# A new fixed order of steps for the opening of a fused attention and feed-forward kernel

## The chip, the cores and the metric

The kernel runs on one core of one Trainium2 chip. A core has TensorE (PE in the profile; its weight loads are shown apart as PEld), VectorE (DVE), ScalarE (ACT), GpSimd (POOL), and SyncE (SP), whose queue issues most of the transfers here. Each engine takes its instructions in order and waits on semaphores for the others. The metric is the device time of one execution in microseconds.

## The reference

```
def _attn_ref(q, k, v):                      # 8 batches, 8 heads, 576 positions, 64 wide
    scores = scale * np.matmul(q, k.transpose(0, 1, 3, 2))
    ...
    masks = np.stack([mask_local if h < H // 2 else mask_strided for h in range(H)], axis=0)
    scores = np.where(masks[None, :, :, :], scores, -1000000000.0)
    ...
    attn = attn / (np.sum(attn, axis=-1, keepdims=True) + 1e-09)
    return np.matmul(attn, v).astype(np.float32)

def _moe_ref(x, w1, w2, w3, w_out):          # x: 4608 tokens x 512; w1..w3: 512 x 768; w_out: 768 x 512
    h = np.maximum(np.maximum(x @ w1, x @ w2), x @ w3)
    return (h @ w_out).astype(np.float32)
```

Half of the heads attend to the last 32 positions, the other half to the positions that agree modulo 32. The result, with the heads side by side, is the `x` of a feed-forward block whose hidden value is the maximum of three products.

## The kernel before

The attention is done in 32 units: a unit is one batch and one pair of heads, in the order strided, strided, local, local. The feed-forward block is done in nine chunks of 512 tokens. A float32 product is made of three products of parts that PE reads faster (`float32r`): every operand is split into a high part and a low rest, for `x` and the hidden value as for the weights. The weights come as pairs of 32-bit words (the host gives float64) and are converted on the chip, in 24 tiles (three matrices by six column blocks, then six of `w_out`).

Up to the end of chunk 0 the order of all work is fixed by a table, `OPENING`. Each entry is a letter and a number, and the steps are recorded on their engines in the order of the table; `pin` keeps that order. The letters:

- **S** n: scores of unit n on PE (lines 248 and 266). **X** n: mask and minus the maximum, DVE (289, 290). **E** n: exponential, ACT (294). **N** n: sums, reciprocal, product and transpose, five instructions on DVE (302 to 307).
- **V** n: value products of unit n on PE into the PSUM tile `o_ps` (lines 333 and 374). **H** n: its high part, copied from `o_ps` by ACT (391) into `xh`. **L** n: its rest, DVE (395), into `xl`. Units 0 to 3 make the `x` of most of chunk 0 (batch 0); 4 to 7 belong to batch 1.
- **A** n: first step of the conversion of weight tile n, two ACT instructions (146, 147) into a tile `work`, of which there are three, and one on POOL (148). **B** n: three DVE instructions (160, 163, 166); the first writes two of the four banks of `o_ps`, in columns that the value products don't use, and the second reads them. **C** n: ACT makes the high part (174), POOL the low one by subtraction (175), which ends the use of `work`.
- **F** n: one of 18 input products of chunk 0 on PE, 12 matmuls (line 410) into one of two banks `f_ps`; weight tile n is needed. **M** n: what takes its result out of the bank: a copy on ACT (421) for every third n, a maximum on DVE (423) for the others, and after the third a cast on ACT (426) and a subtraction on POOL (427). F n + 2 waits for M n.
- **O** n: one of four output products, 18 matmuls (436), into the same two banks; **Q** n: copy on ACT and store (441, 442).

The four banks of `o_ps` are shared between V, H, L and B, and accesses by different engines to one bank are kept in the order of the table, whether their columns meet or not.

The 24 loads of weights and the first loads of `q`, `k` and `v` are issued ahead of the table; S n and V n with n of 4 or more issue the loads of unit n + 2. Behind the table, for chunks 1 to 8, a scheduler places the steps.

Of the kernel before, what the change touches and what calls it, by code (L numbers as in the profile page):

```python
# [43 lines left out]


OPENING = """
S0 X0 S1 E0 N0 A0 X1 B0 E1 S2 V0 N1 A1 B1 H0 X2 A2 L0 S3 V1 E2 C0 A3 H1 C1 B2 X3 N2 E3 L1 V2 A4 H2 N3 L2
S4 V3 B3 C2 A5 C3 B4 H3 L3 X4 A6 E4 B5 C4 F0 M0 F1 F2 B6 C5 M1 N4 C6 A7 M2 B7 F3 S5 A8 X5 A9 C7 B8 M3 F4
F5 V4 E5 B9 C8 A10 A11 M4 C9 M5 F6 N5 A12 F7 B10 M6 B11 C10 F8 H4 S6 A13 C11 B12 C12 A14 L4 M7 B13 A15
B14 C13 C14 M8 F9 V5 F10 M9 A16 X6 A17 B15 M10 C15 B16 E6 F11 F12 B17 A18 C16 M11 B18 C17 A19 M12 F13  # L50
A20 C18 A21 N6 F14 M13 B19 S7 B20 H5 C19 F15 C20 M14 F16 M15 B21 A22 F17 L5 A23 M16 C21 B22 C22 M17 V6
B23 X7 C23 O0 Q0 E7 O1 Q1 H6 O2 N7 L6 Q2 V7 H7 O3 Q3 L7
"""


# [518 lines left out]
```

## Time and profile before

| | us |
|---|---|
| median of 3 runs | 737.13 (736.61 to 740.75) |
| profiled execution | 736.63 |
| its span, first to last instruction | 734.9 |
| PE busy | 700.3 (95%) |
| DVE busy | 315.7 (43%) |
| ACT busy | 171.5 (23%) |
| POOL busy | 124.0 (17%) |

The shares are means over a span with two very different parts: the opening, where all engines work on the conversion, the first units and chunk 0, and the rest, where PE is busy without a break. Times below are counted from the span's start.

### The profile page before, as it was taken

The page shows a single profiled execution, that of the slowest core. Times are in us where ns is not written, and L with a number is a line of the kernel's source. Part 1 is how long each engine was busy: PE and PEld are TensorE (multiplying, and loading weights), DVE is VectorE, ACT ScalarE, POOL GpSimd, SP SyncE. Part 2 cuts the span into 40 slices and gives each one's busy share as a digit, 9 for nine tenths or more (in the row PEclk, how much of TensorE's full clock was granted, in tenths as well). Part 3 has the DMA queues.
Part 4 walks back from the last instruction along what each step waited for, and adds up shares of the span by engine and source line. Part 5 has one row for each costly group of instructions (what it writes and reads, how often), then busy time and mean ns, then how long its engine had stood idle before and what let it go on. Part 6 is the DMA issues. An engine that isn't in the chain of part 4 may idle for free.

```text
span 734.9 us, 18756 instructions
## 1 busy us (share of the span) xinstructions
PE 700.3 (95%) x8448; PEld 563.2 (77%) x8448; DVE 315.7 (43%) x527; ACT 171.5 (23%) x346; POOL 124.0 (17%) x129
## 2 busy tenths in 40 slices
PE   6387998999999999999999999999999999999997
PEld 5266766888788887888788878887888788888885
DVE  5677997444425441555145523553344401101110
ACT  2435654222212111122111212121122211111111
POOL 4235665011101110011001100101011101200110
PEclk9999999999999999999999999999999999999999
DMA  8996111311231122222222211222210010000001
GB/s 240 283 312 239 46 40 45 106 54 53 62 120 54 54 62 88 73 66 62 73 68 57 92 58 62 60 75 66 88 54 21 12 48 1 0 29 29 1 1 57
DMA packets 35807, 55.34 MB, mean 75 GB/s; under 512 B 5200, under 2 KB 18512, under 8 KB 35728
## 3 DMA queue, kind: packets, MB, share of 16 engines
q1 hardware_dynamic: 30016, 44.19, 20.5%
q10 hardware_dynamic: 5712, 9.96, 3.7%
q8 instruction: 66, 1.08, 0.6%
q14 instruction: 13, 0.11, 0.0%
HBM read 44.70 MB, written 9.44 MB: 74 GB/s over the span
## 4 chain that ended last, share of the span: by engine, by line
PE 82%; DVE 2%; POOL 1%; issue 1%; ACT 0%; DVEq 0%; POOLq 0%; ACTq 0%
PE f_ps L410 55%; PE f_ps L436 20%; PE s_ps L266 4%; PE o_ps L333 2%; PE o_ps L363 2%; DVE work L166 1%; POOL wNone L175 1%; DVE work L163 0%; DVE o_ps L160 0%; ACT work L441 0%; POOL work L148 0%; DVE h_max L423 0%; DVE s_ps L305 0%; POOL hl L427 0%; DVE s_ps L302 0%
## 5 line engine op out<-in xcount | busy, mean ns | idle before, releaser
L410 PE MATMUL f_ps<-xh,w 128*128 128x512 f32 x1296 | 417.1, 396 | 6.8 <-DVE h_max L423 5.9
L410 PEld LDWEIGHTS f_ps<-xh,w 128*128 128x128 f32 x1296 | 244.9, 189 | 61.7 <-DVE h_max L423 7.4
L410 PE MATMUL f_ps<-xl,w 128*128 128x512 f32 x648 | 254.2, 392 | 0.7 <-DVE xl L395 0.7
L427 POOL TENSOR_TENSOR hl<-h_max,hh 128x512 fp32r<-128x512 f32 x54 | 70.0, 1296 | 534.9 <-ACT hh L426 534.9
L423 DVE TENSOR_TENSOR h_max<-f_ps,h_max 128x512 f32<-128x512 f32 x108 | 74.5, 689 | 187.9 <-PE f_ps L410 187.9
L436 PE MATMUL f_ps<-wNone,hh 128*128 128x512 f32 x432 | 140.9, 396 | 1.8 <-ACT wNone L174 0.7
L410 PEld LDWEIGHTS f_ps<-xl,w 128*128 128x128 f32 x648 | 122.7, 189 | 24.9 <-DVE xl L395 1.0
L436 PEld LDWEIGHTS f_ps<-wNone,hh 128*128 128x128 f32 x432 | 81.0, 188 | 20.5 <-ACT work L441 1.3
L436 PE MATMUL f_ps<-wNone,hl 128*128 128x512 f32 x216 | 85.0, 394 | 0.0
L426 ACT CAST hh<-h_max 128x512 fp32r<-128x512 f32 x54 | 33.5, 621 | 205.7 <-DVE h_max L423 205.7
L395 DVE TENSOR_TENSOR xl<-o_ps,xh 128x320 fp32r<-128x320 f32 (+11 forms) x96 | 28.3, 350 | 80.0 <-ACT xh L391 80.0
L441 ACT COPY work<-f_ps 128x512 f32<-128x512 f32 x36 | 20.9, 586 | 123.9 <-PE f_ps L436 123.9
L266 PEld LDWEIGHTS s_ps<-qk_t 64*32 64x32 f32 x3200 | 35.1, 111 | 18.6 <-issue 16.6
L421 ACT COPY h_max<-f_ps 128x512 f32<-128x512 f32 x54 | 31.7, 587 | 74.7 <-PE f_ps L410 43.0
L436 PEld LDWEIGHTS f_ps<-wNone,hl 128*128 128x128 f32 x216 | 40.6, 188 | 8.1
L266 PE MATMUL s_ps<-qk_t 64*32 64x18 f32 (+1 forms) x3200 | 40.8, 209 | 3.7 <-DMA qk_t<-in_kT 2.0
L294 ACT ACTIVATE s_ps<-s_ps 128x640 f32<-128x640 f32 (+2 forms) x32 | 20.3, 635 | 85.6 <-DVE s_ps L290 85.1
L287 DVE TENSOR_TENSOR s_ps<-s_ps,mpair 128x576 f32<-128x576 f32 x12 | 9.2, 767 | 67.8 <-PE s_ps L266 67.8
L333 PEld LDWEIGHTS o_ps<-pt,v_t 32*64 32x64 f32 x1344 | 18.5, 141 | 19.3 <-DVE xl L395 10.4
L333 PE MATMUL o_ps<-pt,v_t 32*64 32x64 f32 (+1 forms) x1344 | 22.0, 238 | 10.8 <-DVE xl L395 10.3
L391 ACT CAST xh<-o_ps 128x320 fp32r<-128x320 f32 (+11 forms) x96 | 24.4, 330 | 32.9 <-PE o_ps L333 25.4
L307 DVE STREAM_TRANSPOSE pt<-s_ps 128x640 f32<-128x640 f32 (+2 forms) x32 | 31.3, 979 | 0.7
(49 smaller groups left out, 341.9 us busy)
## 6 DMA issues: line engine op xcount, KB each, us to landing
out<-work ACTq DMA_DIRECT2D x36, 256.0 KB
w<-in_w SPq DMA_DIRECT2D x17, 512.0 KB
qk_t<-in_qT SPq DMA_DIRECT2D x28, 288.0 KB
qk_t<-in_kT SPq DMA_DIRECT2D x28, 288.0 KB
v_t<-in_v_str SPq DMA_DIRECT2D x48, 128.0 KB
v_t<-in_v_loc SPq DMA_DIRECT2D x48, 96.0 KB
wNone<-in_w_out SPq DMA_DIRECT2D x6, 512.0 KB
v_t<-in_v_str SPq DMA_DIRECT2D x16, 72.0 KB
```

Source lines behind the costliest of these rows:

```text
L266: pin(nc.tensor.matmul(s_ps[32 * j : 32 * (j + 1), h, k1 : k1 + w], t[hs, q0 : q0 + 32], t[hs, k0 : k0 + w], start=not first, stop=not fir ...
L307: pin(nc.vector.transpose(pt[:, :, : nm * at], s_ps[:, :, : nm * at]))
L333: pin(nc.tensor.matmul(o[h * D : (h + 1) * D, j, 32 * max(m, 0) : 32 * max(m, 0) + width], v[js, h, m + 1, :], pt[js, h, m * TK + 32 : m * ...
L391: pin(nc.scalar.copy(out=hi, in_=src))
L395: pin(nc.vector.tensor_tensor(out=lo, in0=src, in1=hi.bitcast(F32), op=ALU.subtract))
L410: pin(nc.tensor.matmul(f_ps, w[:, kc, :], x[:, kc, :], start=(kc == 2 and n == 0), stop=(kc == 1 and n == 2)))
L421: pin(nc.scalar.copy(out=a, in_=f_ps))
L423: pin(nc.vector.tensor_tensor(out=a, in0=f_ps, in1=a, op=ALU.max))
L426: pin(nc.scalar.copy(out=hh, in_=a))
L427: pin(nc.gpsimd.tensor_tensor(out=hl, in0=a, in1=hh.bitcast(F32), op=ALU.subtract))
L436: pin(nc.tensor.matmul(f_ps, h[:, ts], w, start=(j == 0 and n == 0), stop=(j == NJ - 1 and n == 2)))
L441: pin(nc.scalar.copy(out=o_sb, in_=hs.pop((c, "out", t))))
```

## The change

The table `OPENING` gets a new order. The steps are the same, each once, and so are their instructions; nothing else in the file differs.

```
 OPENING = """
-S0 X0 S1 E0 N0 A0 X1 B0 E1 S2 V0 N1 A1 B1 H0 X2 A2 L0 S3 V1 E2 C0 A3 H1 C1 B2 X3 N2 E3 L1 V2 A4 H2 N3 L2
-S4 V3 B3 C2 A5 C3 B4 H3 L3 X4 A6 E4 B5 C4 F0 M0 F1 F2 B6 C5 M1 N4 C6 A7 M2 B7 F3 S5 A8 X5 A9 C7 B8 M3 F4
...
+A0 S0 X0 E0 N0 S1 X1 B0 E1 S2 A1 N1 C0 X2 V0 A2 B1 B2 H0 C1 S3 A3 L0 X3 V1 E2 E3 N2 C2 H1 L1 V2 N3 A4 S4
+H2 A5 L2 B3 C3 X4 E4 B4 C4 V3 H3 N4 L3 F0 A6 B5 A7 F1 C5 B6 M0 C6 M1 A8 S5 B7 X5 C7 A9 B8 E5 F2 F3 C8 M2
...
 """
```

In the part that is not printed, V4 to F6 read `V4 E5 B9 C8 A10 A11 M4 C9 M5 F6` before, and now `V4 A10 A11 M3 F4 B9 C9 B10 F5 C10 H4 M4 A12 S6 M5 X6 A13 F6`. M8 to F11 read `M8 F9 V5 F10 M9 A16 X6 A17 B15 M10 C15 B16 E6 F11` before, and now, from V5 on, `V5 A15 A16 F9 M8 B14 C14 B15 A17 B16 M9 C15 B17 A18 C16 A19 F10 M10 F11`. The last conversion, `B23 ... C23`, and O0 read `V6 B23 X7 C23 O0` before, and now `M17 B23 X7 C23 H6 O0`. On PE the same blocks follow each other up to F1; from there S5 stands before F2 and no longer before F4, S6 before F6 and no longer before F9.

How the order stands on the engines at three places. First DVE early in the fill, where the pair of line 395 is L0 and the three with `w_0_185` around it are B2:

```order
-L395 TENSOR_TENSOR xl<-o_ps,xh 128x512
-L395 TENSOR_TENSOR xl<-o_ps,xh 128x64
 L160 TENSOR_SCALAR o_ps<-work 128x2x256
 L163 SCALAR_TENSOR_TENSOR work<-w_0_185,o_ps 128x512
 L166 ISA work<-w_0_185,work 128x1024
+L395 TENSOR_TENSOR xl<-o_ps,xh 128x512
+L395 TENSOR_TENSOR xl<-o_ps,xh 128x64
```

L0 stood ahead of B2 and now stands behind it.

Then DVE later in the fill, with B3 (its last row first), B4 (`w_1_195`), the three rows of L3 and, with line 289 and 290, X4:

```order
 L166 ISA work<-w_1_193,work 128x1024
+L289 TENSOR_REDUCE mx<-s_ps 128x16
+L290 TENSOR_TENSOR s_ps<-s_ps,mx 128x2x8x18
 L160 TENSOR_SCALAR o_ps<-work 128x2x256
 L163 SCALAR_TENSOR_TENSOR work<-w_1_195,o_ps 128x512
 L166 ISA work<-w_1_195,work 128x1024
-L395 TENSOR_TENSOR xl<-o_ps,xh 128x480
-L395 TENSOR_TENSOR xl<-o_ps,xh 128x32
-L395 TENSOR_TENSOR xl<-o_ps,xh 128x64
-L289 TENSOR_REDUCE mx<-s_ps 128x16
-L290 TENSOR_TENSOR s_ps<-s_ps,mx 128x2x8x18
```

X4 now stands ahead of B4; L3 stands further on, behind the five instructions of N4, and V3 is recorded behind B4 and no longer ahead of B3.

Last DVE about V4, with B9 (`w_3_213`) behind B8 (its last row first), and M4 and M5 as the two of line 423:

```order
 L166 ISA work<-w_2_211,work 128x1024
-L160 TENSOR_SCALAR o_ps<-work 128x2x256
-L163 SCALAR_TENSOR_TENSOR work<-w_3_213,o_ps 128x512
-L166 ISA work<-w_3_213,work 128x1024
-L423 TENSOR_TENSOR h_max<-f_ps,h_max 128x512 x2
+L423 TENSOR_TENSOR h_max<-f_ps,h_max 128x512
 L302 TENSOR_REDUCE s_ps<-s_ps 128x2x8
```

B9 no longer stands here between B8 and a maximum: the one row of line 423 is M2, and M4 and M5 come later, behind B9 and B10.

## Rows read from the trace of the kernel before

**Rows 1.** Busy time by stretch: length, busy us of each engine, clock, DMA share, GB/s
```profile
core 0: us, PE busy (x) PEld busy (x) DVE busy (x) ACT busy (x) POOL busy (x), PEclk, DMA share, GB/s
0.00:44.41 44.41, 24.01 (x973) 19.18 (x973) 24.98 (x47) 14.30 (x28) 14.36 (x36) 1.00 0.92 277
50.58:117.72 67.14, 59.88 (x830) 47.15 (x828) 59.78 (x90) 39.10 (x71) 42.14 (x40) 0.97 0.32 111
117.72:138.77 21.05, 19.70 (x289) 15.43 (x284) 9.88 (x19) 6.35 (x16) 3.82 (x3) 1.00 0.30 89
138.77:734.90 596.13, 591.63 (x6360) 477.97 (x6352) 215.20 (x362) 109.24 (x226) 61.77 (x48) 1.00 0.18 54
```

**Rows 2.** Who PE waited for, 0 to 138.77 us: total, times, longest
```profile
PE f_ps L410 <- DVE h_max L423: 5.9, 5, 3.0
```

**Rows 3.** Timeline of the fill: start, us, engine, line, instructions, idle before and releaser
```profile
20.66 0.70 ACT L391 CAST xh<-o_ps 128x512 fp32r<-128x512 f32 x2 [1.66 <-DVE work L163]
...
22.68 0.67 ACT L146 ACTIVATE work<-w 128x512 f32<-128x512 f32 x1 [1.32 <-DMA w<-in_w]
...
23.42 0.61 POOL L148 TENSOR_SCALAR work<-work 128x512 f32<-128x512 f32 x1 [4.30 <-ACT work L146]
...
23.78 2.22 PE L374 MATMUL o_ps<-pt,v_t 18*64 18x18 f32 x128 [1.89 <-DVE xl L395]
...
28.69 0.69 DVE L160 TENSOR_SCALAR o_ps<-work 128x512 int32<-128x512 int32 x1 [4.96 <-ACT xh L391]
...
32.53 0.82 DVE L302 TENSOR_REDUCE s_ps<-s_ps 128x10 f32<-128x640 f32 x1
...
35.49 0.78 DVE L395 TENSOR_TENSOR xl<-o_ps,xh 128x512 fp32r<-128x512 f32 x2
...
36.33 1.65 PE L333 MATMUL o_ps<-pt,v_t 32*64 32x64 f32 x84 [10.32 <-DVE xl L395]
...
39.29 1.33 PE L248 MATMUL s_ps<-mstr,unit 128*128 128x144 f32 x4 [1.31 <-DVE pt L307]
...
42.83 1.65 PE L333 MATMUL o_ps<-pt,v_t 32*64 32x64 f32 x84
...
45.43 1.05 PE L410 MATMUL f_ps<-xh,w 128*128 128x512 f32 x2
...
49.21 0.87 DVE L395 TENSOR_TENSOR xl<-o_ps,xh 128x480 fp32r<-128x480 f32 x3
...
50.01 0.50 PE L410 MATMUL f_ps<-xl,w 128*128 128x512 f32 x1 [0.67 <-DVE xl L395]
...
50.35 0.62 PE L410 MATMUL f_ps<-xh,w 128*128 128x512 f32 x2
...
51.04 0.62 PE L410 MATMUL f_ps<-xh,w 128*128 128x512 f32 x2
```

**Rows 4.** Timeline around V4 and F6
```profile
67.34 1.44 PE L374 MATMUL o_ps<-pt,v_t 18*64 18x18 f32 x128
...
68.89 0.69 DVE L160 TENSOR_SCALAR o_ps<-work 128x512 int32<-128x512 int32 x1 [3.60 <-PE o_ps L374]
...
70.44 0.69 DVE L166 CUSTOM_DVE_ANT_0 work<-w,work 128x1024 uint16<-128x1024 uint16 x1
...
71.05 1.41 DVE L423 TENSOR_TENSOR h_max<-f_ps,h_max 128x512 f32<-128x512 f32 x2
...
71.79 0.77 PE L410 MATMUL f_ps<-xh,w 128*128 128x512 f32 x1 [3.01 <-DVE h_max L423]
```

**Rows 5.** Busy time by stretch, behind the longest wait of PE
```profile
71.85:75.25 3.40, 3.40 (x8) 2.72 (x9) 3.23 (x8) 1.87 (x3) 3.14 (x3) 0.50 0.23 62
```

**Rows 6.** Timeline and, last, group of line 166 on DVE, 0 to 138.77 us
```profile
97.04 1.28 POOL L175 TENSOR_TENSOR w<-work,w 128x512 fp32r<-128x512 f32 x1 [0.46 <-ACT w L174]
...
97.35 1.51 DVE L166 CUSTOM_DVE_ANT_0 work<-w,work 128x1024 uint16<-128x1024 uint16 x1
...
L166 DVE CUSTOM_DVE_ANT_0 work<-w,work 128x1024 uint16<-128x1024 uint16 x18 | 17.8, 989 | 2.0
```

More of the change, by code (lines that the diff above doesn't have):

```diff
@@ L46 @@
 OPENING = """
-S0 X0 S1 E0 N0 A0 X1 B0 E1 S2 V0 N1 A1 B1 H0 X2 A2 L0 S3 V1 E2 C0 A3 H1 C1 B2 X3 N2 E3 L1 V2 A4 H2 N3 L2
-S4 V3 B3 C2 A5 C3 B4 H3 L3 X4 A6 E4 B5 C4 F0 M0 F1 F2 B6 C5 M1 N4 C6 A7 M2 B7 F3 S5 A8 X5 A9 C7 B8 M3 F4
[L49 to L52, printed above, removed]
+A0 S0 X0 E0 N0 S1 X1 B0 E1 S2 A1 N1 C0 X2 V0 A2 B1 B2 H0 C1 S3 A3 L0 X3 V1 E2 E3 N2 C2 H1 L1 V2 N3 A4 S4
+H2 A5 L2 B3 C3 X4 E4 B4 C4 V3 H3 N4 L3 F0 A6 B5 A7 F1 C5 B6 M0 C6 M1 A8 S5 B7 X5 C7 A9 B8 E5 F2 F3 C8 M2
+N5 V4 A10 A11 M3 F4 B9 C9 B10 F5 C10 H4 M4 A12 S6 M5 X6 A13 F6 B11 B12 F7 M6 C11 L4 F8 C12 B13 E6 M7 A14
+C13 V5 A15 A16 F9 M8 B14 C14 B15 A17 B16 M9 C15 B17 A18 C16 A19 F10 M10 F11 C17 B18 F12 C18 M11 H5 M12
+N6 F13 A20 F14 L5 A21 B19 V6 C19 A22 M13 F15 B20 C20 M14 F16 M15 A23 F17 B21 M16 B22 C21 C22 S7 M17 B23
+X7 C23 H6 O0 E7 L6 N7 O1 Q0 O2 V7 Q1 H7 L7 O3 Q2 Q3
 """
```

## The prediction

> **What bounds the kernel now.** I read first the busy time in stretches cut at three events on PE: the first matmul of F0 (44.41 us), the first of F1 (50.58) and the first of O0 (117.72), with chunk 1 starting at 138.77 [rows 1]. From 138.77 to the end PE is busy for 591.6 of 596.1 us: nothing in this table of steps touches that part, because the program behind it is the same. So the change is worth what it takes from, or adds to, the 138.77 us before it, and it can do so only through the time in which PE waits, or runs slowly. PE's work is a fixed sum.
>
> Three parts of it are to be seen. In the fill (0 to F0) PE is busy for 24.0 of 44.4 us. From F1 to O0 it is idle for 67.14 - 59.88 = 7.26 us, and of these the list of waits gives 5.9 us, in five waits, to the running maximum M on DVE (line 423), which hands back one of the two banks of `f_ps` [rows 2]. From O0 to chunk 1 it is idle for 21.05 - 19.70 = 1.35 us.
>
> The timeline shows why. The value products V, their copies H and L, and the middle step of a weight conversion, B, share one PSUM tile, `o_ps`, and wait for each other in the order in which the table names them. H0 on ACT started at 20.66, released by line 163 of B1, although B1 has nothing to do with head pair 0; B2 on DVE stood from 23.7 to 28.69 waiting for the copies H1 that V1 has to precede [rows 3]. DVE is in order, so X3, N2 and L1 stood behind B2, and V2 on PE waited 10.32 us for L1. The same at V3: its products began at 42.83 and took 1.65 us, but B3 and B4 stand between V3 and L3, so the last operand of F0 was written from 49.21 on, and F0's matmul with it started at 50.01 [rows 3].
>
> **The change, part by part.** I walk the new order with the old durations. The loads are issued in the same order up to the last weight, so I keep their landings: the DMA share of the fill is 0.92 [rows 1], and no step moved there issues a load.
>
> *Fill.* B2 now stands ahead of H0. Its weight lands at 22.68 (A2 starts then, released by the DMA), POOL is done at 24.03 [rows 3]. B2's first two instructions, 0.69 each with small gaps, take 1.45: 25.5. H0 0.70: 26.2. L0 0.78: 27.0, so V1 starts near 27.1, which is 3.3 us *later* than its 23.78. But then nothing is in the way: behind L0 come X3 and N2. From B2's start at 28.69 to N2's start at 32.53 are 3.84 us and N2 lasts until 35.49, 2.96; in the new order B2 starts at 24.06, so N2 starts at 24.06 + 3.84 + 0.78 = 28.7 and ends at 31.6. V1 (2.22) and H1 end by 30.1 and are hidden. L1 0.78: V2 at 32.45 instead of 36.33, 3.9 us earlier. N3 follows (as long as N2), to 35.3, and frees the scores' bank for S4, which with its sequel took 42.83 - 39.29 = 3.54: 38.85. B3 fits in before that. X4, two of the five instructions of a block like N2 and on fewer columns, I take as 0.9; the first two parts of B4 are 1.45: 41.2. V3 waits for these, 41.25 to 42.8, and F0 starts at 42.8 instead of 44.41, **1.6 us** earlier. V3 is followed at once by H3 (0.7), and L3 comes behind N4 on DVE (41.9 plus at most N2's 2.96, plus L3's 0.87: 45.7). F0 needs L3 for its 11th matmul. In the old run a pair of F0's first matmuls took 1.05 us, against 0.62 for a pair from 50.35 on, where three starts are 0.69 apart, 0.23 each [rows 3]: that is the 1.2 GHz level, though the clock column has no record that early, with 0.43 a matmul (8 in 3.40 us) [rows 5]. I let the slow part last 3.5 us again, as behind the longest wait below: 8 matmuls until 46.3, four at 0.23 follow, and L3 is early. F1 starts at 47.3 instead of 50.58: **-3.3 us**, bounds -1.6 (only F0's start moves) and -4.
>
> *F1 to O0.* Work of PE here: 59.88, less what a slow clock cost. At 71.85 to 75.25 the granted clock is 0.50 (1.2 GHz), right behind the longest wait, with 8 matmuls in it [rows 5]; half of 3.40 is 1.7. So 58.2 at full clock. The longest wait, 3.01 us, is one chain: V4 on PE, 67.34 to 68.78; B9 on DVE waits for it, 68.89 to 71.13; the maximum M4, the first of the two of line 423, stands behind B9 and ends near 71.74; F6 needs the bank that M4 frees, 71.79 [rows 4]. In the new order M3 stands ahead of B9, and F4, F5 and S6 come between V4 and F6. Between V4 and F6 PE then has two F of 2.75 (12 times 0.23) and a score block (S4's 3.54 at the slow level, so about 1.8), over 7 us, against two conversions of 2.2 (68.89 to 71.05) to 2.7 and M4's 0.7 on DVE: covered, the wait goes to 0, and the clock should stay at 2.4 GHz. If that cover were gone, it would cost what it costs now, 3.0 + 1.7. S5 likewise goes between F1 and F2, about 1.8 us of PE work while DVE does B5 and the first maximum. What is late next: the new table lets M9 stand behind A17 on ACT, A17 behind C14 on POOL (three buffers named `work`), C14 behind the subtraction of M8, while PE has V5, F9 and F10 in that time. That is a series of about 0.7 (M8), 0.7 (its cast), 1.3 and 1.3 (two subtractions on POOL [rows 6]), 1.3 (A17, two of 0.67 [rows 3]) and 0.6 us (M9) and queueing, against about 7 of PE. I expect a wait ahead of F11 between 0 and 3.0 (the longest of its kind now) and take 2.4, and five small ones of 0.25 at V5, F9, F12, F13 and F15. Sum 3.65. 58.2 + 3.65 = 61.85 instead of 67.14: **-5.3 us**, bounds 0 (the idle time and the clock drop come back at other places) and -8.9 (all idle time and the clock's loss go).
>
> DVE must be able to follow: it has 59.78 busy us in the old stretch. In the new order N4 (at most 2.96) and B5 (2.2) are done before F1, so about 55 of 61.85: it fits, at 90%.
>
> *O0 to chunk 1.* The last conversions, B23 and C23, now stand before O0; the waits for them (1.35) go: **-1.3 us**, bounds 0 and -1.3.
>
> Sum: -3.3 - 5.3 - 1.3 = -9.9. The profiled execution has 736.63 us with a span of 734.90; 725.0 of span gives 726.7, and the median of the runs lies 0.5 above the profiled one: **727.2 us**.
>
> **The rule weighed against it.** The third instruction of B, line 166, takes 0.69 alone [rows 4], 0.99 on average over 18 of 24, and 1.51 where it starts inside a POOL subtraction: POOL 97.04 to 98.32, DVE 97.35 to 98.86, so it ends 0.54 after POOL does [rows 6]. The Trainium skill, page "SBUF — State Buffer", section "Who interferes with whom", says that VectorE and GpSimd share a pair of ports as an exclusive lock, and whoever issues second is fully blocked. The trace agrees here. By that rule the new order, which lets B follow on B with a C in between, might have every line 166 wait out a subtraction: I price this as the fourth rival, from the rows.
>
> **The rivals.**
> 1. *The waits only move.* The fill's gain stays, but DVE, ACT and POOL queues give PE as much to wait for from F1 on as now. For it: DVE at 90%, and M9 behind A17. Against it: the longest wait has a plain cause that the new order undoes. 737.1 - 3.3 = 733.8.
> 2. *Slower: the late V1 carries through.* If all behind V1 depends on V1 rather than on DVE, its 3.3 us stay: 737.1 + 3.3 = 740.4. The point that decides is whether V2 starts later than 36.33. Against it: V2 waited 10.32 us for DVE, not for V1, which ended at 26.0.
> 3. *No wait at F11*: 727.2 - 2.4 = 724.8. For it: the series and PE's work are about equal.
> 4. *The lock.* 18 times 1.51 - 0.99 adds 9.4 to DVE's 55 from F1 to O0: 64.4, past 61.85 by 2.5: 729.7. Against it: C's cast and subtraction are about 0.7 and 1.28 behind one line 166, and two of 0.69 stand ahead of the next, so a held one loses about 0.5, not 0.8.
>
> **How the numbers follow.** Chances: the forecast 0.66 (own range 725 to 730; its upper part has a clock drop at F11, 1.7 as above), waits only move 0.12, slower 0.05, no wait at F11 0.09, lock 0.08. The range 723.5 to 732.5 leaves out the slower case and most of rival 1. Half a per cent, 3.7 us, is about what a measurement of this kernel can tell from no change: faster is below 733.4. Forecast, 3, 4 and about half of rival 1 are faster, 0.89; the rest of rival 1 and a little of 2 the same, 0.07; slower 0.04.
>
> **What would show it.** Right: V1 near 27, V2 near 32.5, F0 near 43 and F1 near 47; no PE wait of 3 us from F1 to O0 but one up to 3 ahead of F11; no half clock after the start of the F steps; chunk 1 near 129. Wrong: V2 after 36, F0's 11th matmul waiting for L3, DVE without idle time from F1 to O0 and line 166 near 1.5 on average, or a half clock behind the wait at F11.

## The result, and the profile after

The changed kernel takes 729.33 us (median of 4 runs, 728.72 to 730.34) against 737.18 for the kernel before beside it: a ratio of 0.9885, with a 95% interval of 0.986 to 0.991. That is 2.1 us above the predicted 727.2 and inside its range. The profiled execution took 728.72 us with a span of 727.0, so 7.9 us of span are gone where 9.9 were forecast.

The busy time of the changed kernel in the same four stretches as [rows 1], cut at F0, F1, O0 and the start of chunk 1:

```profile
core 0: us, PE busy (x) PEld busy (x) DVE busy (x) ACT busy (x) POOL busy (x), PEclk, DMA share, GB/s
0.00:46.87 46.87, 21.88 (x972) 17.72 (x973) 30.90 (x58) 15.96 (x31) 15.69 (x38) 0.73 0.90 270
50.66:111.80 61.14, 58.12 (x830) 46.06 (x828) 56.00 (x84) 37.82 (x68) 40.36 (x39) 1.00 0.39 129
111.80:131.17 19.37, 19.37 (x288) 15.49 (x285) 8.12 (x17) 5.10 (x14) 2.75 (x3) 1.00 0.30 99
131.17:727.00 595.83, 591.63 (x6359) 477.83 (x6352) 215.18 (x362) 109.20 (x226) 61.78 (x48) 1.00 0.18 54
```

Set beside the sum of the prediction:

| stretch | before | after | change | predicted |
|---|---|---|---|---|
| start to F1 | 50.58 | 50.66 | +0.1 | -3.3 |
| F1 to O0 | 67.14 | 61.14 | -6.0 | -5.3 |
| O0 to chunk 1 | 21.05 | 19.37 | -1.7 | -1.3 |
| chunk 1 to the end | 596.13 | 595.83 | -0.3 | 0 |

The two stretches behind F1 gave a little more than forecast; the whole miss is in the fill, which gave nothing, outside the bounds of -1.6 to -4 that it had been given. F0 starts at 46.87 and not at 42.8. What PE waited for up to chunk 1 says where to look (in all, times, longest):

```profile
PE s_ps L266 <- issue: 6.3, 3, 4.4
PE o_ps L374 <- DVE xl L395: 6.1, 1, 6.1
PE o_ps L333 <- DVE xl L395: 3.3, 1, 3.3
...
PE o_ps L333 <- DVE work L163: 2.4, 1, 2.4
PE f_ps L410 <- ACT h_max L421: 1.9, 1, 1.9
PE o_ps L333 <- issue: 1.4, 1, 1.4
PE f_ps L410 <- DVE h_max L423: 0.7, 1, 0.7
```

The 10.3 us of V2 [rows 3] have become 6.1 at V1 and 3.3 at V2, the five waits for the running maximum [rows 2] one of 0.7 and one of 1.9 for M9 (predicted: 2.4 ahead of F11). But the top row has no engine to blame: for 4.4 us at a stretch PE stood in the middle of a step while it waited for nothing that the profile shows. The timeline of the fill, with the rows that answer to V2, S4 and V3 in [rows 3]:

```profile
31.87 1.26 PE L333 MATMUL o_ps<-pt,v_t 32*64 32x64 f32 x59 [3.29 <-DVE xl L395]
...
34.58 0.67 PE L333 MATMUL o_ps<-pt,v_t 32*64 32x64 f32 x25 [1.45 <-issue]
35.18 1.33 PE L248 MATMUL s_ps<-mstr,unit 128*128 128x144 f32 x4
...
36.89 1.16 PE L266 MATMUL s_ps<-qk_t 64*32 64x18 f32 x98 [0.38 <-DMA qk_t<-in_kT]
...
42.41 0.44 PE L266 MATMUL s_ps<-qk_t 64*32 64x18 f32 x30 [4.36 <-issue]
42.96 0.46 DVE L289 TENSOR_REDUCE mx<-s_ps 128x16 f32<-128x288 f32 x1 [3.69 <-PE s_ps L266]
...
45.29 1.65 PE L333 MATMUL o_ps<-pt,v_t 32*64 32x64 f32 x84 [2.44 <-DVE work L163]
```

V2 began at 31.87, 4.5 us earlier than before (forecast: 3.9). It broke off after 59 of its 84 passes, and S4 after 98 of 128; X4 on DVE stood 3.69 us for it, then B4, V3 and F0. Between the two breaks lie 25 + 4 + 98 = 127 passes, and a pass is two instructions, a weight load and a matmul. In the kernel before, S4 broke off after the same 98 passes, for 0.74 us.

The trace has an instruction queue (q8) whose packets are 16 KB each. Over the whole execution q8 has 66 packets, and PE has 8448 matmuls, each with a weight load: 128 pairs of instructions to a packet. In e1_pad below, with 64 more, there are 67. So the queue is taken here as the one that brings PE's instructions. The transfers in two stretches of the changed kernel, 33.2 to 39.7 us (the first row; no packet of q8 in it) and 39.7 to 41.1 us (the other two): packets, MB, share of the 16 engines' time.

```profile
q1 hardware_dynamic: 1580, 1.69, 111.1%
...
q1 hardware_dynamic: 484, 0.48, 104.2%
q8 instruction: 1, 0.02, 5.0%
```

The trace also has the time of each packet, which the view above doesn't print. PE went on 1.3 to 1.7 us behind the end of one in each of these breaks (two experiments of the next section are added):

```
kernel, break         packet (us)      PE goes on
before, S4 pass 98    39.93 to 41.05   42.46
after,  V2 pass 59    31.94 to 33.04   34.58
after,  S4 pass 98    39.84 to 40.96   42.41
e1_pad, V1 pass 123   33.78 to 34.91   36.60
e2_paced, S4 pass 98  36.77 to 39.43   40.74
```

So the theory, called the supply theory below: PE's instructions come in blocks of 16 KB, 127 or 128 of these small passes each; entering one block asks for the next, and while the loads fill the DMA engines it takes 5 to 8 us from there until PE can go on (7.8 from 34.58 to 42.41), though PE runs through a block in some 3.5. Before, V2's wait of 10.32 us for DVE gave the fetch its time. With that wait gone, the fetch is what is late next. The Trainium skill, page "Runtime: NRT & Kernel Launch", section "Instruction fetch mechanics", says that the sequencer fetches the next block of 16 KiB (256 instructions) through its own DMA queue while it runs the current one, and that the cost is mostly hidden. The trace agrees on the block; here it isn't hidden.

### The profile page after: what moved, and what is told of

Its sections match the earlier page's. It is cut to its first block, busy times and chain, and to the rows that moved or that the text cites. A ratio compares the mean times of both kernels' runs of the same rounds, so it can differ in the third digit from the quotient of the medians.

```text
span 727.0 us, 18760 instructions
## 1 busy us (share of the span) xinstructions
PE 694.8 (96%) x8448; PEld 560.2 (77%) x8448; DVE 313.8 (43%) x527; ACT 171.1 (24%) x346; POOL 123.0 (17%) x129
## 4 chain that ended last, share of the span: by engine, by line
PE 86%; DVE 1%; ACT 0%; issue 0%; DVEq 0%
PE f_ps L410 57%; PE f_ps L436 21%; PE s_ps L266 4%; PE o_ps L333 2%; PE o_ps L363 2%; ACT work L441 0%; DVE work L163 0%; DVE h_max L423 0%; PE s_ps L248 0%; DVE o_ps L160 0%; DVE work L166 0%; DVEq L166 0%; DVEq L160 0%
```

## The experiments

Every time stands beside the kernel before, run on the same chip; its medians there were 736.6 to 738.1, so the ratios are the numbers to compare. They lie up to 0.002 from the quotient of the two medians, so small differences of medians and of ratios do not agree in all rows.

| run | median, us | ratio to before (95%) |
|---|---|---|
| the change | 729.33 | 0.9885 (0.986 to 0.991) |
| e1_pad | 729.47 | 0.9885 (0.986 to 0.9911) |
| e2_paced | 734.65 | 0.9945 (0.9927 to 0.9963) |
| e3_new_fill | 735.57 | 0.9963 (0.9948 to 0.9977) |
| e4_new_rest | 734.82 | 0.9964 (0.9944 to 0.9985) |
| e5_old_m4 | 734.17 | 0.9971 (0.9955 to 0.9987) |
| e6_new_m9 | 734.08 | 0.9961 (0.9943 to 0.9979) |
| e7_staged | 725.22 | 0.984 (0.9816 to 0.9864) |
| e8_staged_m9 | 728.72 | 0.989 (0.9869 to 0.9911) |
| e9_old_staged | 736.25 | 0.9986 (0.9973 to 0.9999) |
| e10_old_fill_staged | 731.61 | 0.9928 (0.9903 to 0.9952) |
| e11_staged_m10 | 726.31 | 0.9843 (0.982 to 0.9867) |
| e12_lock | 727.62 | 0.9869 (0.9844 to 0.9895) |

**e1_pad: do the breaks sit at fixed instructions?**

```diff
-        for m in range(0 if b >= PAIRED else MS):
+        extra = [0, 1, 2, 3] if n == 0 else []
+        for m in range(0) if b >= PAIRED else [*extra, *range(MS)]:
```

> The new kernel, with the first 32 products of V0 recorded twice (64 more passes of PE, 128 instructions; the second writing gives the same values). Supply theory: PE's instructions arrive in blocks of 16 KB, one block covers about 127 small float32 passes, and PE stands in S4 (from 38.05 to 42.41 us) because the next block is not there. The extra passes shift the block's edges by half a block: the break after the 98th pass of S4 goes, another appears about 34 passes into S4 or at another place of the fill, S4 is done near 38 to 40 instead of 42.85, F0 starts 1 to 4 us before 46.87, and the time falls by 1 to 4 us to 725.3 to 728.3. Rival, a wait for data or for an engine that the profile does not name: S4 breaks off after the same pass at the same time, 42.4, and the time is 729.3 to 730 (0.3 us of added products).

The timeline of PE, with its passes in V0, V1, S4 and V3:

```profile
24.19 1.06 PE L375 MATMUL o_ps<-pt,v_t 18*64 18x18 f32 x56 [3.94 <-issue]
...
30.64 2.00 PE L375 MATMUL o_ps<-pt,v_t 18*64 18x18 f32 x123 [0.46 <-DVE xl L396]
36.60 0.41 PE L375 MATMUL o_ps<-pt,v_t 18*64 18x18 f32 x5 [3.96 <-issue]
...
42.88 1.65 PE L266 MATMUL s_ps<-qk_t 64*32 64x18 f32 x128
46.91 0.85 PE L333 MATMUL o_ps<-pt,v_t 32*64 32x64 f32 x34 [2.38 <-DVE work L163]
49.04 1.15 PE L333 MATMUL o_ps<-pt,v_t 32*64 32x32 f32 x50 [1.28 <-issue]
```

With 64 passes more in V0, the edges of the blocks fall 64 passes earlier in the steps behind it: V2's from its pass 59 to pass 123 of V1, where PE now stands for 3.96 us, and S4's from its pass 98 to pass 34. There S4 runs through: PE had waited 1.66 us ahead of V2 and 1.30 us ahead of S4 for DVE, and the packet was in at 41.27. The next edge, 94 + 34 = 128 passes on, is at pass 34 of V3, and there PE stands again. So the breaks belong to places in the instruction stream, not to data or a point in time. The expected gain did not come. The breaks only moved, two of nearly 4 us now stand in V0 and V1, and the ratio is that of the change. The profiled execution is the slowest of six (734.48 us), so breaks as long as these are not what the median of 729.47 has. What is short is the rate of supply, not one unlucky block.

**e2_paced: is it the loads?** Tiles 6 to 23 and unit 5 are held until DVE has done N3.

```diff
-... V2 N3 A4 S4
+... V2 N3 W0 A4 S4
+            if hold and n == 0:
+                pin(nc.vector.memset(raw[:, 0:1], 0))
...
-    load_weights(5)
+    load_weights(3)
...
+    def late_loads():
+        load_weights(3, hold=True)
+        load_qk(5)
+        load_v(5)
+        load_weights(len(sources))
```

> The new kernel, with the loads of weight tiles 6 to 23 and of unit 5 held back until DVE has done N3 (near 35 us), by a one-column write on DVE into the buffer of the first held load; no other step moves. Supply theory: the block of instructions that PE lacks in S4 travels through the same transfer engines as the loads, 5 to 8 us while they are full; without the held loads it comes by about 36, the break in S4 falls from 4.36 to under 1.5 us, F1 starts near 47 instead of 50.66, and the time falls by 2 to 4 us to 725.3 to 727.3, unless the late weights make A and B of tiles 6 to 8 late (then the gain is seen in F0 and lost again before F6). Rival, the break has nothing to do with transfers: it stays at 4.4 us and the time is 729.3 or more.

The break in S4; and, as busy times by stretch with clock, DMA share and GB/s last, the time from PE's entry into the block before that break (V2 pass 59) to the start of the next packet:

```profile
40.74 0.44 PE L268 MATMUL s_ps<-qk_t 64*32 64x18 f32 x30 [2.65 <-issue]
...
34.83:36.77 1.94, 1.78 (x29) 1.52 (x29) 1.17 (x3) 1.17 (x4) 0.00 (x0) 0.50 0.01 2
```

The break fell from 4.36 to 2.65 us and F1 started at 49.35, 1.3 us earlier, less than expected: the held loads began to move just when the packet did, so it still took 2.65 us, from 36.77. It also started 1.9 us after the entry although the DMA share was 0.01 in between, so not all of the delay is the loads'. All 18 tiles in one go then held up the loads of unit 6 behind them; PE waited 5.33 us for them in S6, and the time is worse than that of the change. The mechanism stood, the edit was bad.

**e3_new_fill and e4_new_rest: the halves alone.** The table is spliced at F0: what stands before it from the one order, the remaining steps in the order of the other.

> The new order up to F0, the old order of what is left behind it. Supply theory: the fill's gain is eaten by the break in S4, so this is worth nothing, F1 near 50.6 and 736.5 to 737.5 us. Theory of the prediction: the fill is worth 3.3 us, 733.5 to 734.

> The old order up to F0, the new order of what is left behind it. Supply theory: the rest is worth all that was gained, 7.9 us, so 729 to 730. Rival: the rest draws on the fill, in which N4, and the conversions ahead of F1, are now done earlier on DVE: without that DVE hands its work on later, and half or less is kept, 732 to 735.

The stretch F1 to O0 of e3:

```profile
50.75:116.60 65.85, 59.32 (x830) 47.08 (x828) 53.99 (x81) 38.30 (x69) 41.12 (x39) 0.97 0.35 120
```

And of e4:

```profile
50.65:114.60 63.95, 61.31 (x830) 47.89 (x828) 60.16 (x91) 39.77 (x72) 42.16 (x41) 0.95 0.35 122
```

With the new fill F1 starts at 50.75, against 50.58 before: the fill by itself gives nothing up to there, as the supply theory has it. The time, 735.57, lies between the two expectations. The rest of e3 is 1.3 us shorter than the 67.14 before; that N4 and B5 are off DVE's list by then fits this, but wasn't tested alone. By medians e3 gained 2.5 us, which the one profile shows only in part. For e4 my expectation of 729 to 730 fell and the rival held: 734.8, with a wide spread of 731.8 to 740.1. Behind the old fill the new rest takes 63.95 and not 61.14 us in the profile, which is e4's fastest execution: S5 stands right behind F1 now and waits 0.94 us for N4, and the granted clock is 0.95 on average. The gain of the rest hangs on work that the new fill does earlier, so the two halves' gains do not add up to the whole.

**e5_old_m4: the longest wait by itself.**

```diff
-F5 V4 E5 B9 C8 A10 A11 M4 C9 M5 F6 ...
+F5 V4 E5 C8 A10 A11 M4 M5 B9 C9 F6 ...
```

> The old order with one place of it changed: M4 and M5 stand ahead of B9 and C9, not behind them. My account of the rest of the opening: the 3.01 us ahead of F6 and the half clock behind them go as soon as M4 no longer stands behind B9; about 2.2 + 1.7 us, 733.4 to 735 for a kernel before of 737 to 738. Rival: DVE is late anyway and the wait comes back ahead of F7 to F11, no change.

The 3.01 us ahead of F6 [rows 4] are gone, so M4's place behind B9 was their cause. In this profile 2.56 us came back ahead of the F step behind S6 (at 82.93), for a maximum on DVE, and the granted clock of 86.50 to 110.00 was 0.93. So the rival, too, is borne out in part. The 2.6 us by medians are within what was expected; how much of the wait is removed for good isn't settled by it.

**e7_staged: loads in three groups, unit 6 not behind them.**

```diff
-H2 A5 L2 B3 C3 X4 E4 ... A8 S5 ... A12 S6
+H2 A5 L2 B3 C3 X4 W0 E4 ... A8 W1 S5 ... A12 W2 S6
...
+    def late(n):
+        if n == 0:
+            load_weights(2, hold=True)
+            load_qk(5)
+            load_v(5)
+            load_weights(4)
+        else:
+            load_weights(6, hold=True)
```

> The new kernel with the loads of weight tiles 6 to 23 held back in three groups of six (released behind X4, A8 and A12; unit 5's loads go with the first group), each by a one-column write on DVE into the buffer of its first load. Supply theory: PE's next block of instructions then comes within about 2 to 3 us instead of 5 to 8 while PE is in V2 and S4; the breaks in V2 and S4 fall from 1.45 and 4.36 us to under 0.7 and 1.5, F0 starts near 43.5 instead of 46.87 and F1 near 47; no weight is late; 725 to 727. If the first held tiles land late, 0.5 to 2 us of this are lost ahead of F1 to F3. Rival, the break is not a matter of the transfers: S4 done at 42.8 as now, 729.5 or more.

PE in the fill, V1 to F0:

```profile
27.09 2.04 PE L376 MATMUL o_ps<-pt,v_t 18*64 18x18 f32 x128 [5.96 <-DVE xl L397]
32.34 1.65 PE L335 MATMUL o_ps<-pt,v_t 32*64 32x64 f32 x84 [3.22 <-DVE xl L397]
35.31 1.33 PE L250 MATMUL s_ps<-mstr,unit 128*128 128x144 f32 x4 [1.31 <-DVE pt L309]
36.57 1.46 PE L268 MATMUL s_ps<-qk_t 64*32 64x18 f32 x128
40.57 1.65 PE L335 MATMUL o_ps<-pt,v_t 32*64 32x64 f32 x84 [2.54 <-DVE work L165]
42.15 0.80 PE L412 MATMUL f_ps<-xh,w 128*128 128x512 f32 x1
```

Its transfers from 33 to 36 us:

```profile
q1 hardware_dynamic: 138, 0.26, 26.1%
q8 instruction: 1, 0.02, 2.4%
```

And its stretches F1 to O0, and O0 to chunk 1:

```profile
47.16:108.32 61.16, 58.11 (x829) 46.03 (x827) 55.22 (x84) 37.31 (x67) 39.79 (x39) 1.00 0.56 178
108.32:127.71 19.39, 19.37 (x288) 15.48 (x284) 8.15 (x17) 5.11 (x14) 2.78 (x3) 1.00 0.30 100
```

Both breaks are gone; the longest that is left, 1.54 us in S3 at 20.22, stands where the loads that aren't held still fill the DMA (a share of 0.90 from 13.0 to 17.3). With the DMA at a share of 0.26 instead of 1.11, the block that S4 ends with came from 34.30 to 35.46, not from 39.84 to 40.96. F1 starts 3.5 us earlier, and behind it everything takes as long as in the change (61.16 and 19.39 us): the 3.3 us between the ratios 0.9885 and 0.984 (0.0045 of 737) are the fill's.

**e9_old_staged and e10_old_fill_staged: the controls.** The same held loads, in the order before, and in the order of e4.

> The kernel before with the loads held back in the same three groups (released behind L2, A8 and A12). Supply theory: the old fill loses only 0.74 us to PE's instructions, since V2 waits 10.3 us for DVE while the next block comes; so the held loads are worth 0 to 0.8 us, 736 to 737 for a kernel before of 737. Rival, fewer transfers at a time make the opening faster whatever the order: 3 us as in the new order, 734 or less.

> Old order up to F0, new order behind it, loads held back as above. If the fill of the prediction is worth its 3.3 us once PE has its instructions, and the rest draws 2.8 us more from it (F1 to O0 took 63.9 us behind the old fill and 61.1 behind the new one), this is 731 to 732 against 725.2 with the new fill. Rival: with the loads held back the fill's order makes no difference, 725 to 728.

Both came out as the supply theory said: 736.25 and 731.61. Held loads alone are worth 0.3 us by medians and 1.0 by the ratio (0.1 to 2.0) with the old order, whose fill hardly runs short; with them, the new fill is worth 731.6 - 725.2 = 6.4 us over the old one with the same rest. F1 stands at 48.77 in the profile of e10, its fastest execution, and at 50.75 in that of e9, against 47.16, so the old fill varies by 2 us here; F1 to O0 takes 64.40 in e10 against 61.16. The waits of e10 show what the old fill leaves undone for the new rest, N4 ahead of S5 (second row, 2.5 us in one):

```profile
PE o_ps L335 <- DVE xl L397: 9.4, 1, 9.4
PE s_ps L250 <- DVE pt L309: 4.0, 3, 2.5
```

**e6_new_m9, e8_staged_m9, e12_lock, e11_staged_m10: the wait ahead of F11.**

```diff
-... A17 B16 M9 C15 B17 A18 C16 A19 F10 M10 F11 ...
+... M9 A17 B16 C15 B17 A18 C16 A19 F10 M10 F11 ...
```

This is e6, on the new order; e8 has the same move on e7.

> The new order with M9 ahead of A17 and B16, not behind them. Account of the prediction: the wait ahead of F11 (1.85 us) hangs on the copy of M9, which stands behind A17 on ACT; it goes, and the time falls by 1.5 to 2 us below the new kernel's 729.4. Rival: A17 and what follows it come later, so the wait moves to F12 or F13, no change.

> The two last edits together. If both are worth what they promise, 723.5 to 725.5; if only the staged loads count, as with these alone; if the DVE and ACT queues set the time from F1 to O0, the earlier F1 turns into waits there and this is 727 to 729.

The wait ahead of F11 went, and one of 4.8 us ahead of F12 came, with a granted clock of 0.58 in the 3.5 us behind it: the move costs 3.5 us with the held loads and more without them. The rival of e6 had named F12, and the 728.7 of e8 lies in the third of its ranges; that the wait grows, and that the time gets worse, neither expectation had. In e8 the rows of B16 and C15, and F12:

```profile
83.94 1.28 POOL L177 TENSOR_TENSOR w<-work,w 128x512 fp32r<-128x512 f32 x1 [0.44 <-ACT w L176]
84.09 1.67 DVE L168 CUSTOM_DVE_ANT_0 work<-w,work 128x1024 uint16<-128x1024 uint16 x1
...
89.55 0.50 PE L412 MATMUL f_ps<-xh,w 128*128 128x512 f32 x1 [4.81 <-DVE h_max L425]
```

The last instruction of B (line 166 before, 168 here) starts 0.15 us behind POOL's subtraction and takes 1.67 us, and the next one 1.60; in e7 both take 0.69:

```profile
84.49 0.69 DVE L168 CUSTOM_DVE_ANT_0 work<-w,work 128x1024 uint16<-128x1024 uint16 x1
...
86.71 0.69 DVE L168 CUSTOM_DVE_ANT_0 work<-w,work 128x1024 uint16<-128x1024 uint16 x1
```

With M9 out of the way ACT casts C15 earlier, so POOL starts first. To test that, e12 puts E6 on ACT between A17 and C15.

```diff
-... E6 M7 A14 C13 V5 ... M9 A17 B16 C15 ...
+... M7 A14 C13 V5 ... M9 A17 B16 E6 C15 ...
```

> As the last but one (loads held back, M9 ahead of A17), with the exponentials E6 on ACT moved from ahead of M7 to between A17 and C15, so that C15's cast and POOL's subtraction start about 0.7 us later, behind the start of B16's line 166 and no longer ahead of it. If the slowdown by M9 comes from line 166 being held by POOL's subtraction: the additions of B16 and B17, 1.67 and 1.60 us, go back to 0.69, the wait of 4.8 us ahead of F12 to about 3.3, no half clock or a short one, 725 to 727. Rival, the slowdown comes from the order of M9 and A17 itself: 728 to 729 as before, with the wait at 4.8.

The same three rows in e12:

```profile
86.10 0.69 DVE L168 CUSTOM_DVE_ANT_0 work<-w,work 128x1024 uint16<-128x1024 uint16 x1
...
86.59 1.33 POOL L177 TENSOR_TENSOR w<-work,w 128x512 fp32r<-128x512 f32 x1 [1.08 <-ACT w L176]
...
89.66 0.50 PE L412 MATMUL f_ps<-xh,w 128*128 128x512 f32 x1 [2.87 <-DVE h_max L425]
```

DVE starts first and both additions take 0.69; the wait is 2.87 us and the clock stays at 1.00. From V5 to F12 it is 12.92 us against 14.83 in e8, and 12.92 in e7. So the hold by POOL was the cause of 1.9 of the 4.8 us at this place. The whole is 727.62 against 728.72 us, less than expected, and the intervals of the two ratios overlap, so a gain of the whole isn't shown. In the profile of e12 two breaks for "issue" are back in the fill (0.75 and 1.01 us), which may have taken some of it.

The last of the four, e11, is e7 with another move:

```diff
-... C15 B17 A18 C16 A19 F10 M10 F11 ...
+... C15 A18 C16 A19 F10 M10 B17 F11 ...
```

> The new order with the loads held back and M10 ahead of B17 on DVE. The wait of 0.78 us ahead of F12 goes: 724.4 to 725. Rival: B17 and C17 come 0.7 us later and line 166 falls into POOL's subtractions, as with M9 moved: 726 to 729.

The wait ahead of F12 went, as it should, and the time didn't: 0.9843 against 0.984. Its profile, the slowest of five executions, has a break of 3.08 us for "issue" in S3, and 0.55 of the clock in the 3.4 us behind F11's wait; neither comes from line 166, so the rival's reason isn't borne out either. The fastest versions are e7 and e11, which these runs can't tell apart; e7 was compared with the change through the kernel before, not side by side.

## Why the prediction came out as it did

**The fill, -3.3 us: the step that failed.** Its part up to V2 was right: V1 at 26.59 (27.1), V2 at 31.87 (32.45). The step that failed is "S4, which with its sequel took 3.54: 38.85": it took 7.67, to 42.85, and V3 and F0 went with it. I carried a duration over without asking what it was made of. It held a break of 0.74 us that ended in "issue", the visible end of a fetch that V2's long wait covered; I had named every engine as the next to be late, but not PE's own supply. e7 shows that nothing else of size was wrong there: with the blocks in time, V1, V2, the end of S4, V3, F0 and F1 stand at 27.09, 32.34, 38.03, 40.57, 42.15 and 47.16, against 27.1, 32.45, 38.85, 41.25, 42.8 and 47.3. That F1 is met to 0.14 us is partly luck: S4 with its sequel took 2.7 instead of 3.54 there, and F0 5.0 instead of 4.5. That the time of the change lies in its range has some luck too: the stretches behind F1 gave 1.4 us more than forecast and made up for part of the fill.

**F1 to O0, -5.3 us: right, -6.0.** The longest wait and the half clock [rows 5] are gone; PE is busy for 58.12 us (58.2 assumed), and the waits left are 1.85 ahead of F11 (2.4 taken), 0.73 and 0.28, instead of 3.65 in all. The 1.8 us for a score block are met (S5 takes 1.85, from 53.38 to 55.23), but by luck: S4's 3.54, which I halved, held the break, and without it the half would be 1.4. The account "N4 and B5 are done before F1" weighed more than I gave it: e4 and e10 lose about 3 us behind the old fill, where DVE has this work still ahead of it.

**O0 to chunk 1, -1.3 us: right,** -1.7: PE has no idle time there.

**The rivals.** Waits that only move: not from F1 on. The late V1: no, V2 is far ahead of 36.33. No wait at F11: it is there. The hold of line 166 by POOL: on average 0.85 us over the same 18, less than the 0.99 before and far from 1.51, so only single ones are held in the change (1.55 us at 84.92); but it is real, and e6 and e8 woke it by moving one copy of 0.6 us. There the trace agrees with the lock of the Trainium skill, page "SBUF — State Buffer", section "Who interferes with whom": the one that starts second is held.

## What to carry to other kernels

When a wait is removed, ask also what the waiting engine's own instruction stream does in that time: a break in a step that ends in "issue", however short, can be a supply that is only just covered; here many small instructions beside loads that filled the DMA made it the next bound. Loads that aren't needed yet can be held back to let the instruction blocks through, in groups small enough that later loads don't queue behind them. Where two engines hold each other by who starts first, a move of half a microsecond on a third engine can cost several, so the order is tested and not only reasoned.

## What the runs showed of the hardware that was not expected

- A 16 KB block of PE's instructions started 5.3 us after PE entered the block before it (34.58 to 39.84) at a DMA share of 1.11, and 1.0 us after in e7 (33.29 to 34.30), at 0.26. The loads are not the whole of it: with a share of 0.12 or less in between, this delay was 0.6 to 1.1 us at seven such edges of V2 and S4 (e7 to e12), but about 2 us in V2 of e2 and of e12; with the loads at 0.9 or more it was 1.6 to 5.3 us at the edges of V1, V2 and S4. What makes up the rest stays open. PE went on 1.3 to 1.7 us behind the packet's end.
- These breaks differ between executions and kernels of nearly the same fill: in e7, e11 and e12, with the same loads and the same table up to F0, the longest was 1.5, 3.1 and 1.1 us. Part of the spread of the medians is likely theirs, which wasn't tested.
- A half clock didn't follow from the length of a wait alone. The granted clock fell to a half behind waits of 3.01 (before), 4.81 (e8) and also 1.83 us (e11), and stayed at full behind 2.87 us (e12) and 1.82 us (e7). In e4 it was at a half from 83.82 to 87.23 us, where the last wait ahead of it, at V5 (81.39), was 0.55 us. What decides it stays open.
